# A retention kernel whose state product runs in 64x64 quarters of the array, with the state evicted by one instruction

## The chip, the cores and the metric

The kernel runs on one core of one Trainium2 chip. The metric is device time in microseconds (us); three runs of the kernel before gave 316.77, 317.41 and 318.12, so the median is 317.41 us. One further execution was profiled. All single durations below come from that execution.

## The reference

For 8 batches (B) and 8 heads (H), with 576 positions (S) and a head size of 64 (D), the reference computes decayed attention without a softmax and then an MLP with a cosine gate:

```python
scores = q @ k.T / sqrt(D)
Dmat   = where(i >= j, gamma[h] ** (i - j), 0)     # gamma[h] = 1 - 2**(-5-h)
ret    = (scores * Dmat) @ v                        # (B, H, S, D)
x      = ret.transpose(0, 2, 1, 3).reshape(4608, 512)
h      = x @ w_in                                   # 512 -> 2048
out    = (h * cos(h)) @ w_out                       # 2048 -> 512
```

Inputs and output are float32; the kernel multiplies in bfloat16 and accumulates in float32.

## The kernel before, in words

**Retention in chunks.** The decay factor of a pair (i, j) splits into a factor of i times a factor of j. The factor of j is multiplied into v when v is cast (tile VB, line 308), the factor of i into the result when it leaves PSUM (tile UP, line 476). Between the two the work is plain linear attention in chunks of 128 positions: r = 0 to 3 with 128 positions and r = 4 with 64. For each batch b and chunk r:

- `scores(b, r)`, line 405: 8 matmuls, one for each head, k against q with a contraction of 64. The two heads of a pair stand on partitions 0 to 63 and 64 to 127 (hp = 0 and 1), so their matmuls use the two row halves of the array (form 64\*128; for r = 4 it is 64\*64). They write two PSUM banks SC. VectorE then multiplies by the causal mask into RT (`mask`, line 426, instruction at line 428).
- `rest(b, r)`, line 433: for r > 0 first the product of the state S (the sum of k^T v over the earlier chunks of the batch) with q, then the 8 matmuls of RT with VB, both into bank PO; for r < 4 then 8 matmuls that add this chunk's k^T v to bank ST (lines 459 to 468), and ScalarE's eviction of ST into the bfloat16 tile SB (lines 469 to 474), which the next chunk's `rest` reads. VectorE moves PO, times UP, into XT (line 476), the transposed input of the MLP.

**The state in SB before.** SB is 128 partitions by 4 pairs of 128 columns. A pair's 128x128 block is block diagonal: head 0's 64x64 state top left, head 1's bottom right, and zeros elsewhere, set once at the start by two memsets (line 236). One matmul with contraction 128 and 128 output partitions (form 128\*128) so serves both heads of a pair: 4 matmuls for each `rest` with r > 0. There are 32 of those: 24 with 128 columns of q (r = 1 to 3) and 8 with 64 (r = 4). The eviction takes two ScalarE instructions of 64 partitions by 256 elements, one for each diagonal.

**The MLP.** Tokens go in 9 blocks j of 512. `mlp1(j, dt)` (line 489) makes one of 16 tiles of h with 4 matmuls of 512 columns; ScalarE takes the cosine into CB (line 504) and VectorE the product into GT (line 507). `mlp2(j, st, part)` (line 514) is one quarter of an output tile, again 4 matmuls of 512 columns; ScalarE evicts the finished tile (line 538) and issues its store. `mlp1` and `mlp2` take turns in four PSUM banks MM.

**The order.** It is written out by hand in `emit` (line 550), and each engine runs its instructions in that order. The helper classes add a semaphore wait where one engine reads what another wrote. PE's instructions are issued by `group` (line 396), so all matmuls have the lines 401 and 403 (the last one of a group, which raises the semaphore) and are told apart by their tiles: `po<-kqt,sb` is the state product, `po<-rt,vb` the product with RT, `st<-vb,kqb` the state's update, `sc<-kqt` the scores, `mm<-xt,win` mlp1, `mm<-wout,gt` mlp2. Waits of a group stand before its first matmul.

- Batch 0 runs at the start, while weights still arrive: `scores` and `rest` for r = 0 to 3 at lines 592 to 609, with `spin` matmuls (of the identity, result unused) between them, r = 4 inside `mlp1(0)` (lines 612 to 619). The pieces of w_in come by POOL's DMA queue; `mlp1(0)` waits for the piece that it reads (dt 0, 2, 4, 8, 12).
- Batch 1 runs inside `mlp2(0)` and `mlp1(1)` (lines 626 to 653). There the `mlp1` tiles have 320 columns at first and 192 after that.
- From j = 1 on (line 654), with b = j + 1: ahead of `mlp2(j)` stands `rest(b-1, 4)`, then `scores(b, 0)`; ahead of its quarters n = 3, 6, 9 and 12 stands `stage(b, r)`, which is `rest(b, r)` and `scores(b, r+1)` for r = 0 to 3. `mlp1(j)` for j > 1 has no retention work of PE. For j = 7, `rest(7, 4)` is the last retention work, with no scores after it; j = 8 has none.

Of the kernel before, what the change touches and what calls it, by code (L numbers as in the profile page):

```python
# [9 lines left out]
BF16 = mybir.dt.bfloat16  # L10
# [113 lines left out]
class _Kernel:  # L124
    def __init__(self, nc, es, q, k, v, w_in, w_out, out):
        self.nc, self.es = nc, es
        self.src = {"q": q.tensor, "k": k.tensor, "v": v.tensor}
        self.w_in, self.w_out, self.out = w_in.tensor, w_out.tensor, out.tensor
        gam = [1.0 - 2.0 ** (-5.0 - h) for h in range(H_)]
        self.lng = [math.log(g) for g in gam]  # L130
        self.s = Sched(nc, es)

        def sb(name, shape, dt):
            return nc.alloc_sbuf_tensor(name, shape, dt)


        self.KQT = [sb(f"kqt{i}", [128, TP], BF16) for i in range(2)]
        self.bQT = [[Buf() for _ in range(NCH)] for _ in range(2)]
        self.bKT = [[Buf() for _ in range(NCH)] for _ in range(2)]
        self.XT = sb("xt", [128, NP * XR], BF16)  # L140
        self.bXT = [Buf() for _ in range(XR // GR)]
        self.WIN = sb("win", [128, 4 * DFF], BF16)
        self.bWIN = [Buf() for _ in range(len(WI) - 1)]
        self.WOUT = sb("wout", [128, 16 * DM], BF16)
        self.bWOUT = [Buf() for _ in range(NWO)]
        self.ST32 = {x: [sb(f"{x}n{r}", [128, DM], F32) for r in range(NCH)] for x in "kv"}
        self.QN = sb("qn", [128, NCH * DM], F32)
        self.bQN = [Buf() for _ in range(NP)]
        self.bST32 = {x: [Buf() for _ in range(NCH)] for x in "kvq"}
        self.bQB = [[Buf() for _ in range(NCH)] for _ in range(2)]  # L150

        self.QX = [sb(f"qx{i}", [128, NP * S_], BF16) for i in range(2)]
        self.bQX = [Buf(), Buf()]
        self.bQ0 = [Buf() for _ in range(NP)]

        self.KQB = [[sb(f"kqb{i}_{r}", [128, 2 * DM], BF16) for r in range(NCH)] for i in range(2)]
        self.bKB = [[Buf() for _ in range(NCH)] for _ in range(2)]
        self.VB = [[sb(f"vb{i}_{r}", [128, DM], BF16) for r in range(NCH)] for i in range(2)]
        self.bVB = [[Buf() for _ in range(NCH)] for _ in range(2)]
        self.RT = [[sb(f"rt{i}_{hp}", [128, 512], BF16) for hp in range(2)] for i in range(2)]  # L160
        self.bRT = [[Buf() for _ in range(2)] for _ in range(2)]
        self.SB = [sb(f"sb{i}", [128, NP * 128], BF16) for i in range(2)]
        self.bSB = [Buf() for _ in range(2)]
        self.GT = [sb(f"gt{i}", [128, 16 * TB], BF16) for i in range(2)]
        self.bGT = [[Buf() for _ in range(16)] for _ in range(2)]
        self.CB = [sb(f"cb{i}", [128, TB], BF16) for i in range(3)]
        self.bCB = [Buf() for _ in range(3)]
        self.n_cb = 0
        self.NOSB = 4
        self.OSB = [sb(f"osb{i}", [128, DM], F32) for i in range(self.NOSB)]  # L170
        self.bOSB = [Buf() for _ in range(self.NOSB)]
        self.n_osb = 0
        self.IG = sb("ig", [128, S_], F32)
        self.IP = sb("ip", [128, NCH], F32)
        self.UP = sb("up", [128, NP * S_], F32)
        self.WV = sb("wv", [128, NCH * H_], F32)
        self.MK = sb("mk", [128, CH], BF16)
        self.ID = sb("ident", [128, 128], BF16)
        self.LNG = sb("lng", [128, NP], F32)
        self.JUNK = sb("junk", [128, 1], F32)  # L180
        self.C_LN8 = sb("c_ln8", [128, 1], F32)
        self.C_PIH = sb("c_pih", [128, 1], F32)
        self.bIG, self.bIP, self.bUP, self.bWV, self.bMK, self.bC, self.bID = (Buf() for _ in range(7))

        def ps(name):
            return nc.alloc_psum_tensor(name, [128, 512], F32)

        self.SC = [ps("sc0"), ps("sc1")]
        self.bSC = [Buf(), Buf()]
        self.PO, self.bPO = ps("po"), Buf()  # L190
        self.ST, self.bST = ps("st"), Buf()
        self.MM = [ps(f"mm{i}") for i in range(4)]
        self.bMM = [Buf() for _ in range(4)]
        self.n_mm = 0
        self.later = None
        self.stores = []
        self.fetched = 2 * NCH
        self.rt = {}
        self.open = {}
# [18 lines left out]
    def consts_a(self):  # L218

        s = self.s  # L220
        s.op("pool", lambda e: e.iota(self.IP.ap(), [[CH, NCH]], base=0, channel_multiplier=1,
                                      allow_small_or_imprecise_dtypes=True), writes=[self.bIP])
        for t, b, fill, first, cmp in ((self.ID, self.bID, 1.0, 0.0, ALU.not_equal),
                                       (self.MK, self.bMK, 0.0, 1.0, ALU.is_ge)):
            s.op("dve", lambda e: e.memset(t.ap(), first), writes=[b])
            s.op("pool", lambda e: e.affine_select(t.ap(), t.ap(), pattern=[[1, CH]],
                                                   compare_op=cmp, fill=fill, base=0,
                                                   channel_multiplier=-1), reads=[b], writes=[b])
        for h in range(H_):
            p0 = 64 * (h % 2)  # L230
            s.op("dve", lambda e: e.memset(bass.AP(self.LNG, p0 * NP + h // 2, [[NP, 64], [1, 1]]),
                                           self.lng[h]), writes=[Buf()])
        s.op("dve", lambda e: e.memset(self.C_LN8.ap(), float(math.log(1.0 / 8.0))), writes=[Buf()])
        s.op("dve", lambda e: e.memset(self.C_PIH.ap(), float(math.pi / 2.0)), writes=[self.bC])
        for i in range(2):
            s.op("dve", lambda e: e.memset(self.SB[i].ap(), 0.0), writes=[self.bSB[i]])
        for h in range(H_):
            s.op("act", lambda e: e.activation(
                bass.AP(self.WV, h, [[NCH * H_, 128], [H_, NCH]]), self.IP.ap(), AF.Exp,
                scale=-self.lng[h]), reads=[self.bIP], writes=[Buf()])  # L240
        self.bWV.w = [Tok("act", "act", s.count["act"], {})]
# [188 lines left out]
            bass.AP(self.MK, 0, [[CH, ck], [0, NP], [1, ck]]), ALU.mult),  # L430
            reads=[sc[1], self.bMK], writes=[self.bRT[k][hp]])

    def rest(self, b, r, po=None):

        s, ck, i, q0 = self.s, ck_of(r), b % 2, CH * r
        k = self.rt[b, r]
# [1 line left out]
        mms = []  # L438
        if r:
            sb = self.SB[(r - 1) % 2]  # L440
            mms += [(bass.AP(po, c * CH, [[512, 128], [1, ck]]),
                     bass.AP(sb, c * 128, [[512, 128], [1, 128]]),
                     bass.AP(self.KQT[i], TQ + c * S_ + q0, [[TP, 128], [1, ck]]),
                     dict(start=c == 0, stop=False, skip_group_check=True)) for c in range(NP)]
        for c in range(NP):
            for hp in range(2):
                h = 2 * c + hp
# [9 lines left out]
        if r < NCH - 1:  # L457
            mms = []
            for c in range(NP):
                for hp in range(2):  # L460
                    h = 2 * c + hp
                    mms.append((
                        bass.AP(self.ST, 64 * hp * 512 + c * D_, [[512, 64], [1, D_]]),
                        bass.AP(self.KQB[i][r], h * D_, [[2 * DM, ck], [1, D_]]),
                        bass.AP(self.VB[i][r], h * D_, [[DM, ck], [1, D_]]),
                        dict(start=r == 0 and c == 0, stop=r == NCH - 2 and c == NP - 1,
                             skip_group_check=True)))
            self.group(mms, [self.bKB[i][r], self.bVB[i][r]], [self.bST])
            for hp in range(2):

                s.op("act", lambda e: e.activation(  # L471
                    bass.AP(self.SB[r % 2], 64 * hp * 512 + 64 * hp, [[512, 64], [128, NP], [1, D_]]),
                    bass.AP(self.ST, 64 * hp * 512, [[512, 64], [D_, NP], [1, D_]]), AF.Copy),
                    reads=[self.bST], writes=[self.bSB[r % 2]] if hp else [Buf()])
        t0 = (b * S_ + q0) % XR
        s.op("dve", lambda e: e.tensor_tensor(  # L476
            bass.AP(self.XT, t0, [[NP * XR, 128], [XR, NP], [1, ck]]),
# [72 lines left out]
    def emit(self):  # L550
# [61 lines left out]
        for dt in range(16):  # L612
# [3 lines left out]
            if dt == 4:  # L616
                self.scores(0, 4)
            if dt == 6:
                self.rest(0, 4)

        self.fetch(2)
        for r in range(NCH):
# [31 lines left out]
        for j in range(1, NTB):  # L654
# [5 lines left out]
            for n in range(16):  # L660

                if n == 0 and b <= B_:
                    self.rest(b - 1, NCH - 1)
                if b < B_:
                    if n == 0:
                        self.scores(b, 0)
                    elif n % 3 == 0 and n < 15:
                        self.stage(b, n // 3 - 1)
                self.mlp2(j, n // 4, n % 4)
        self.flush()  # L670
# [31 lines left out]
```

## Time and profile before

| what | value |
|---|---|
| median of three runs | 317.41 us (316.77 to 318.12) |
| the profiled execution: its own time | 316.4 us |
| span of its trace | 314.7 us |
| granted clock of TensorE | 1.0 over the whole span |
| busy: PE, DVE, ACT, POOL | 303.5, 174.1, 162.3, 93.1 us |
| the eviction into SB (line 471) | 64 instructions, 378 ns each |
| state product, 128 columns of q | 92 records, 219 ns each |
| state product, 64 columns of q | 32 records, 193 ns each |

A span on PE is modelled: a matmul's recorded length covers its way through the array, and the next one starts long before it ends. What PE pays for a matmul is therefore read from the distance between starts: 216 ns from one 512-column matmul to the next, 56 ns for 128 columns. In the text, "gap" is such a distance. (Four more state products of 128 columns stand in the trace under the tile `mm`.) Single matmul records are missing from the trace, and such a place shows a gap that is one matmul too long.

### The profile page before, as it was taken

What the parts mean: (1) busy time and instruction counts of PE and PEld (TensorE: products, weight loads), DVE (VectorE), ACT (ScalarE), POOL (GpSimd) and SP (SyncE); (2) the same over time, 40 slices, a digit from 0 to 9 for tenths busy, and PEclk for the clock granted to TensorE, in tenths of its full rate; (3) what the DMA queues carried; (4) which work ended last, traced back from release to release, by engine and by line L of the source; (5) the groups of instructions that cost most, each with busy time, mean ns of one, the idle gap of its engine ahead of it and who ended that gap; (6) DMA issues with size and microseconds to landing.
All of it is one profiled execution on the core that took longest, in us unless ns stands there. A gap on an engine that the chain in (4) does not pass through costs nothing.

```text
span 314.7 us, 6424 instructions
## 1 busy us (share of the span) xinstructions
PE 303.5 (96%) x2516; PEld 159.6 (51%) x2552; DVE 174.1 (55%) x301; ACT 162.3 (52%) x290; POOL 93.1 (30%) x128
## 2 busy tenths in 40 slices
PE   6989999999999999999999999999999999999996
PEld 5754455666544455445544554455444544444442
DVE  3567624787527743685458644765387438405700
ACT  7566525785337533763277236723473257316711
POOL 2692027535454434453445424210000000000000
PEclk9999999999999999999999999999999999999999
DMA  7999999999999999999999999940001100120021
GB/s 218 213 168 204 203 220 247 264 192 209 212 256 183 217 210 247 217 224 217 259 208 202 225 204 221 172 85 35 33 0 38 66 33 0 42 94 1 12 83 74
DMA packets 142814, 48.85 MB, mean 155 GB/s; under 512 B 132544, under 2 KB 137664, under 8 KB 142784
## 3 DMA queue, kind: packets, MB, share of 16 engines
q1 hardware_dynamic: 132320, 34.22, 59.7%
q0 software_dynamic: 5280, 4.78, 9.5%
q10 hardware_dynamic: 5184, 9.44, 8.9%
q8 instruction: 20, 0.33, 0.4%
q14 instruction: 10, 0.08, 0.1%
HBM read 36.70 MB, written 9.44 MB: 147 GB/s over the span
## 4 chain that ended last, share of the span: by engine, by line
PE 90%; DMA 2%; DVE 2%; ACT 2%; issue 2%; SPq 1%; POOL 0%; DVEq 0%
PE mm L401 59%; PE mm L403 20%; PE po L401 6%; PE sc L401 4%; DMA kn<-in_k_dram 2%; PE st L401 1%; DVE gt L507 1%; DVE rt L428 1%; SPq L276 1%; ACT sb L471 0%; DVE xt L476 0%; ACT L604 0%; ACT osb L538 0%; ACT kqt L365 0%; SPq L267 0%
## 5 line engine op out<-in xcount | busy, mean ns | idle before, releaser
L507 DVE TENSOR_TENSOR gt<-mm,cb 128x512 bf16<-128x512 f32 (+2 forms) x160 | 101.1, 637 | 66.2 <-ACT cb L504 63.6
L401 PE MATMUL mm<-xt,win 128*128 128x512 bf16 (+2 forms) x468 | 116.0, 358 | 1.0 <-DVE xt L476 0.3
L504 ACT ACTIVATE cb<-mm,c_pih 128x512 bf16<-128x512 f32 (+2 forms) x160 | 101.9, 645 | 27.8 <-PE mm L403 27.0
L401 PE MATMUL mm<-wout,gt 128*128 128x512 bf16 x408 | 111.8, 380 | 2.3 <-issue 1.7
L401 PEld LDWEIGHTS mm<-xt,win 128*128 128x128 bf16 x480 | 44.6, 98 | 48.8 <-DVE gt L507 2.3
L401 PEld LDWEIGHTS mm<-wout,gt 128*128 128x128 bf16 x432 | 39.3, 98 | 45.1
L403 PE MATMUL mm<-xt,win 128*128 128x512 bf16 (+2 forms) x160 | 57.2, 358 | 0.3
L538 ACT ACTIVATE osb<-mm 128x512 f32<-128x512 f32 x36 | 21.5, 597 | 68.0 <-PE mm L403 68.0
L403 PE MATMUL mm<-wout,gt 128*128 128x512 bf16 x144 | 54.6, 379 | 0.5
L308 POOL TENSOR_TENSOR vb<-vn,wv 128x512 bf16<-128x512 f32 (+1 forms) x40 | 41.7, 1043 | 29.2 <-DMA vn<-in_v_dram 24.7
L428 DVE TENSOR_TENSOR rt<-sc,mk 128x512 bf16<-128x512 f32 (+1 forms) x78 | 45.8, 625 | 4.8 <-PE sc L403 4.8
L476 DVE TENSOR_TENSOR xt<-po,up 128x512 bf16<-128x512 f32 (+1 forms) x39 | 24.7, 634 | 41.9 <-PE po L403 41.8
L471 ACT ACTIVATE sb<-st 64x256 bf16<-64x256 f32 x64 | 24.2, 378 | 40.1 <-PE st L403 38.7
L318 POOL CAST kqb<-kn 128x512 bf16<-128x512 f32 (+1 forms) x40 | 24.4, 611 | 65.2 <-DMA kn<-in_k_dram 56.2
L318 POOL CAST kqb<-qn 128x512 bf16<-128x512 f32 (+1 forms) x30 | 18.5, 615 | 17.7 <-DMA qn<-in_q_dram 17.5
L403 PEld LDWEIGHTS mm<-xt,win 128*128 128x128 bf16 x160 | 15.7, 98 | 15.7
L403 PEld LDWEIGHTS mm<-wout,gt 128*128 128x128 bf16 x144 | 14.1, 98 | 17.0
L401 PE MATMUL po<-rt,vb 128*64 128x128 bf16 (+1 forms) x273 | 15.2, 220 | 0.0
L401 PE MATMUL sc<-kqt 64*128 64x128 bf16 (+1 forms) x273 | 14.7, 215 | 0.0
L401 PEld LDWEIGHTS po<-kqt,sb 128*128 128x128 bf16 x124 | 8.6, 98 | 7.8 <-DVE rt L428 1.6
L401 PEld LDWEIGHTS po<-rt,vb 128*64 128x64 bf16 (+1 forms) x273 | 9.3, 108 | 5.9 <-DVE rt L428 2.1
L401 PE MATMUL po<-kqt,sb 128*128 128x128 bf16 (+1 forms) x124 | 11.2, 213 | 0.4 <-DVE rt L428 0.2
(88 smaller groups left out, 133.2 us busy)
## 6 DMA issues: line engine op xcount, KB each, us to landing
out_dram<-osb ACTq DMA_DIRECT2D x36, 256.0 KB, 3.3
kn<-in_k_dram SPq DMA_DIRECT2D x32, 256.0 KB, 4.7
vn<-in_v_dram SPq DMA_DIRECT2D x32, 256.0 KB, 5.3
qn<-in_q_dram SPq DMA_DIRECT2D x24, 256.0 KB, 4.8
wout<-in_moe_w_out_dram POOLq DMA_DIRECT2D x4, 512.0 KB, 14.5
win<-in_moe_w_in_dram POOLq DMA_DIRECT2D x3, 512.0 KB, 8.2
qn<-in_q_dram SPq DMA_DIRECT2D x4, 288.0 KB, 4.7
kn<-in_k_dram SPq DMA_DIRECT2D x8, 128.0 KB, 3.5
```

Source lines behind the costliest of these rows:

```text
L276: s.dma("sp", f"q0_{c}", lambda e: e.dma_start(dst, src), writes=[self.bQN[c]])
L308: self.s.op(eng, lambda e: e.tensor_tensor(bass.AP(self.VB[i][r], 0, v3), self.staged("v", r, v3[1:]), bass.AP(self.WV, r * H_, [[NCH * H_ ...
L318: self.s.op(eng, lambda e: e.tensor_copy(o, f), reads=[self.bST32[x][r]], writes=[bt[i][r]])
L401: self.nc.tensor.matmul(o, a, b, **kw)
L403: return s.done("pe", self.nc.tensor.matmul(o, a, b, **kw), reads, writes)
L428: self.s.op("dve", lambda e: e.tensor_tensor(bass.AP(self.RT[k][hp], 0, p3), bass.AP(sc[0], 0, p3), bass.AP(self.MK, 0, [[CH, ck], [0, NP] ...
L471: s.op("act", lambda e: e.activation(bass.AP(self.SB[r % 2], 64 * hp * 512 + 64 * hp, [[512, 64], [128, NP], [1, D_]]), bass.AP(self.ST, 6 ...
L476: s.op("dve", lambda e: e.tensor_tensor(bass.AP(self.XT, t0, [[NP * XR, 128], [XR, NP], [1, ck]]), bass.AP(po, 0, [[512, 128], [CH, NP], [ ...
L504: s.op("act", lambda e: e.activation(co, mo, AF.Sin, bias=self.C_PIH.ap(), scale=1.0), reads=[bm, self.bC], writes=[bcb])
L507: s.op("dve", lambda e: e.tensor_tensor(bass.AP(g, dt * TB + o, [[16 * TB, 128], [1, n]]), mo, co, ALU.mult), reads=[bm, bcb], writes=[bg])
L538: s.op("act", lambda e: e.activation(o.ap(), m.ap(), AF.Copy), reads=[bm], writes=[bo])
```

## The change

SB shrinks to 4 pairs of 64 columns: partitions 0 to 63 hold the states of the heads hp = 0, partitions 64 to 127 those of hp = 1, packed side by side, exactly as they lie in ST. So one ScalarE instruction of 128 partitions by 256 elements evicts both, and the two memsets go. The state product becomes 8 matmuls for each `rest` with r > 0, one for each head: contraction 64, 64 output partitions, with hp = 0 in the quarter of rows 0 to 63 and columns 0 to 63 and hp = 1 in the opposite quarter (form 64\*64).

For r = 4, whose RT product uses the rows 0 to 63 with both column halves (64\*64), `rest` gets an argument `mid`: the state product is issued as a group of its own, then `mid()` issues other PE work, then PE waits for its own semaphore until the state product is complete, then the RT product follows. For batches 1 to 6 `mid` is `scores(b, 0)`, which stood after `rest` before; for batches 0 and 7 it is one spin matmul, which is new and takes an MM bank. The group of the state product for r = 4 thus waits only for SB, q and PO; the wait for RT and VB moves behind `mid`. On VectorE, the two masks of `scores(b, 0)` come ahead of the XT instruction of `rest(b-1, 4)` instead of after it.

```diff
-        self.SB = [sb(f"sb{i}", [128, NP * 128], BF16) for i in range(2)]
+        self.SB = [sb(f"sb{i}", [128, NP * D_], BF16) for i in range(2)]
...
-        for i in range(2):
-            s.op("dve", lambda e: e.memset(self.SB[i].ap(), 0.0), writes=[self.bSB[i]])
...
-    def rest(self, b, r, po=None):
+    def rest(self, b, r, po=None, mid=None):
...
-            mms += [(bass.AP(po, c * CH, [[512, 128], [1, ck]]),
-                     bass.AP(sb, c * 128, [[512, 128], [1, 128]]),
-                     bass.AP(self.KQT[i], TQ + c * S_ + q0, [[TP, 128], [1, ck]]),
-                     dict(start=c == 0, stop=False, skip_group_check=True)) for c in range(NP)]
+            mms += [(bass.AP(po, 64 * hp * 512 + c * CH, [[512, 64], [1, ck]]),
+                     bass.AP(sb, 64 * hp * NP * D_ + c * D_, [[NP * D_, 64], [1, D_]]),
+                     bass.AP(self.KQT[i], 64 * hp * TP + TQ + c * S_ + q0, [[TP, 64], [1, ck]]),
+                     dict(start=c == 0, stop=False, skip_group_check=True))
+                    for c in range(NP) for hp in range(2)]
+        if mid:
+            done = self.group(mms, [self.bSB[(r - 1) % 2], self.bQT[i][r]], [bpo])
+            mid()
+            s.eng["pe"].wait_ge(s.sem["pe"], done.val)
+            mms = []
...
-            for hp in range(2):
-                s.op("act", lambda e: e.activation(
-                    bass.AP(self.SB[r % 2], 64 * hp * 512 + 64 * hp, [[512, 64], [128, NP], [1, D_]]),
-                    bass.AP(self.ST, 64 * hp * 512, [[512, 64], [D_, NP], [1, D_]]), AF.Copy),
-                    reads=[self.bST], writes=[self.bSB[r % 2]] if hp else [Buf()])
+            s.op("act", lambda e: e.activation(
+                self.SB[r % 2].ap(), self.ST[:, 0:NP * D_], AF.Copy),
+                reads=[self.bST], writes=[self.bSB[r % 2]])
...
-                self.rest(0, 4)
+                self.rest(0, 4, mid=lambda: self.spin(1))
...
-                    self.rest(b - 1, NCH - 1)
+                    self.rest(b - 1, NCH - 1, mid=(lambda: self.scores(b, 0)) if b < B_
+                              else (lambda: self.spin(1)))
                 if b < B_:
-                    if n == 0:
-                        self.scores(b, 0)
-                    elif n % 3 == 0 and n < 15:
+                    if n % 3 == 0 and 0 < n < 15:
                         self.stage(b, n // 3 - 1)
```

## The prediction

> **What bounds the kernel now.** I read the page first, busy times and chain:
>
> ```profile
> PE 303.5 (96%) x2516; PEld 159.6 (51%) x2552; DVE 174.1 (55%) x301; ACT 162.3 (52%) x290; POOL 93.1 (30%) x128
> PE 90%; DMA 2%; DVE 2%; ACT 2%; issue 2%; SPq 1%; POOL 0%; DVEq 0%
> PE mm L401 59%; PE mm L403 20%; PE po L401 6%; PE sc L401 4%; DMA kn<-in_k_dram 2%; PE st L401 1%; DVE gt L507 1%; DVE rt L428 1%; SPq L276 1%; ACT sb L471 0%; DVE xt L476 0%; ACT L604 0%; ACT osb L538 0%; ACT kqt L365 0%; SPq L267 0%
> ```
>
> PE is busy 96% of the span and 90% of the chain; ScalarE's eviction of the state (ACT sb L471) rounds to 0% of it. What ScalarE saves is then worth something only where PE waits for it; what PE has to do more is paid in full wherever PE runs without a gap. So the next view is PE's timeline of one steady stage, batch 3, r = 2:
>
> ```profile
> 116.87 0.38 PE L403 MATMUL mm<-wout,gt 128*128 128x512 bf16 x1
> 117.09 0.39 PE L401 MATMUL po<-kqt,sb 128*128 128x128 bf16 x4
> 117.41 0.41 PE L401 MATMUL po<-rt,vb 128*64 128x128 bf16 x7
> 117.60 0.22 PE L403 MATMUL po<-rt,vb 128*64 128x128 bf16 x1
> 117.65 0.29 PE L401 MATMUL st<-vb,kqb 128*64 128x64 bf16 x7
> 117.75 0.20 PE L403 MATMUL st<-vb,kqb 128*64 128x64 bf16 x1
> 117.88 0.39 PE L401 MATMUL sc<-kqt 64*128 64x128 bf16 x7
> 118.06 0.22 PE L403 MATMUL sc<-kqt 64*128 64x128 bf16 x1
> 118.21 0.61 PE L401 MATMUL mm<-wout,gt 128*128 128x512 bf16 x2
> ```
>
> The starts of the single records (ns) give gaps. mm to state product 216, the normal 512-column distance: PE waits for nothing, and both have form 128\*128. Inside the state product 56, 55, 56. Then 149 to the first RT product, whose form is 128\*64: 93 more than 56. Inside that, two heads start 3 to 4 apart and pairs follow at 56 (the second pair at 80), 195 from first to last start. st follows at 53 (same form); sc, form 64\*128, at 128 where 28 would follow; mm at 148. So **every change of form costs about 93 to 100 ns**: the next form starts only once the last one is through. The change needs two more rows: form 64\*64 after 128\*128, and form 64\*64 in opposite quarters. The turning of q in batch 1 has both:
>
> ```profile
> 42.85 0.38 PE L403 MATMUL mm<-wout,gt 128*128 128x512 bf16 x1
> 43.16 0.47 PE L401 MATMUL po<-ident,qx 64*64 64x64 bf16 x17
> ```
>
> Gap 309 (216 + 93); inside, the two quarters of a pair start 3 ns apart, the second pair 52 after the first, the others at 32, a 64-column stream's price.
>
> **The change part by part.**
>
> *State product, r = 1 to 3.* Before, from the last mm start to the first RT product: 216 + 167 + 149 = 532. After: mm to 64\*64 309; four pairs at the RT product's own pattern (same columns, also pairs on disjoint column halves) 195; to form 128\*64 149, since that again differs: 653. **+120 ns.** Eight matmuls in pairs take four slots, as four full ones did: the zeros that go were never paid for, and one change of form is added. Batches 2 to 7, 18 times: **+2.16 us**. In batch 1, r = 1 waits 469 for ScalarE's turned k (end 53.65) in bank PO, which hides the change of form: +0.02; r = 2 and 3 wait for their second mask (gap 180, where 136 would be normal) and start at 136 + 93 = 229: +0.07 each. Together **+0.15**.
>
> *r = 4, batches 1 to 6.* Before: 216 + 87 (state) + 123 + 119 (RT) + 125 + 181 (scores) + 148 to the first mm = 999. After: 309 + 119 (state, the 64-column pattern of form 64\*64) + 125 + 181 (scores) + 148 + 119 (RT) + 125 = 1126. +0.127, six times: **+0.76**. That takes the wait for PE's own semaphore as hidden. Behind it on PE stand the RT product and all of mlp2. The state product's end is 193 after its last start; consumers start 58 to 99 after the end they wait for (the state product at 14.517 after the mask's end at 14.459; the one at 19.114 after ScalarE's end at 19.015). So release is at 251 to 292, while scores hold the array until 125 + 181 + 148 = 454: 160 to spare. If PE released only once the scores were through as well, it would be 216 + 58 instead of 148: +0.13 each, +0.76 in all, the upper bound; below nothing it cannot go.
>
> *r = 4, batch 7,* has one spin as cover. Before 216 + 86 + 124 + 119 + 125 = 670; after 309 + 119 + X + 119 + 125 with X between 125 + 149 = 274 (two changes of form) and 292 (the release): **+0.28**. *Batch 0, r = 4* waits today for its second mask (start 27.91, mask's end 27.85). Its state product, freed of that wait, goes ahead at 27.69, the spin at 27.93, RT at about 28.08 against 28.13: 0. The spin's MM bank has been emptied by then (gt of dt = 3 ends at 26.1), and the next tiles find theirs empty too.
>
> *The eviction.* Which form will it cost like? The groups kept apart by form say:
>
> ```profile
> L471 ACT ACTIVATE sb<-st 64x256 bf16<-64x256 f32 x64 | 24.2, 378 | 40.1 <-PE st L403 38.7
> L365 ACT ACTIVATE kqt<-mm 128x256 bf16<-128x256 f32 x2 | 0.8, 376 | 0.0
> ```
>
> Same elements in a partition, twice the partitions, same time: 32 instructions of 0.38 us go, 12 us of ScalarE. In the steady stages SB is ready at about 118.8 for a reader at 120.8: worth 0. It stands on the chain once, at the start (chain in order of time):
>
> ```profile
> 18.34 0.27 ACT sb L471
> 18.61 0.03 issue
> 18.64 0.39 ACT sb L471
> 19.02 0.09 issue
> 19.11 0.72 PE mm L401 x11
> ```
>
> There `rest(0, 3)` would start some 0.37 earlier (from 18.64 the masks, ready at 18.61, are next to be waited for). But what is late next is a DMA: the first piece of w_in lands at 20.41, just ahead of mlp1(0) at 20.64, so at most 0.13 is left there, and the third piece lands at 24.52; PE's wait for it ends, and dt = 4 starts at 24.66:
>
> ```profile
> 24.63 0.34 PEld L401 LDWEIGHTS mm<-xt,win 128*128 128x128 bf16 x3 [0.54 <-DVE gt L507]
> ```
>
> The gt named as releaser can only be the one that ended at 24.05 (the next ends at 24.92), in time for an unhindered start at 24.42; the weights were what came last. POOL issues that piece, and nothing of POOL changes. So the gain ends here: **0**, and the changes of form in batch 0 end here too, with 0.24 to spare. Without this cover it would be -0.37.
>
> *The rest.* The two memsets (272 ns each, until 2.65) precede a VectorE wait for q until 4.78: 0. On VectorE, XT of `rest(b-1, 4)` falls behind two masks and ends at about 109.7 in batch 3's stage, as the second mask does now; the reader of both starts at 109.97, after the change 0.13 later: covered by 0.2. Queues of SP and POOL do not change.
>
> **Sum:** 2.16 + 0.15 + 0.76 + 0.28 = **+3.35 us**. The profiled execution took 316.4 with a span of 314.7; it would be 319.75 and 318.0. That execution lies 1.0 under the median 317.41, to which I add the same: **320.8**.
>
> A page speaks against the pairs: the Trainium skill, "TensorEngine Tiling (Array Packing)", Gotcha 1, says that different row tiles cannot write one PSUM bank at the same time. Both quarters of a pair are different row tiles and write PO. The turning of q also writes one bank from both row halves, in opposite column halves, 3 ns apart, so I go by the row; by the page the time would be the second rival's.
>
> **The rivals.**
>
> 1. *Not slower:* the change of form from 64\*64 to 128\*64 costs nothing. Its place is between state and RT product for r = 1 to 3; both forms share the column halves, and this direction is nowhere in the trace. It would give 56 instead of 149, -93 ns 21 times, -1.95: +1.40, **318.8**, within 0.5%. It decides from a gap of about 65 on. Against it: the opposite direction (st 128\*64 to sc 64\*64, 126 where 28 would follow) pays in full, as does each other pair of forms.
> 2. *Pairs in series.* Eight slots instead of four: about +0.22 for 128 columns, 21 times, +0.10 for 64, 7 times: +5.3 more, **326.1**. Against it the 3 ns above.
> 3. *The own wait exposed:* +0.76, **321.5**. For it: no such wait is in the trace. Against it: 160 ns of cover.
> 4. *The eviction does what it says in time:* the start keeps its 0.37 because w_in lands sooner, **320.4**; or, the change not doing what it says, one eviction costs as much as two: ScalarE keeps its time, and the forecast stays, since nothing rests on it.
>
> **How the numbers follow.** Forecast with rival 4: 0.80; rival 1: 0.08; rivals 2 and 3: 0.05 each; 0.02 is left for what no row shows. The range leaves out rival 2 and takes in 1 and 3 with the spread of the runs shown (0.7 each side of the median): 318.7 to 322.0. 0.5% is 1.6 us, about what a measurement of this kernel can tell from no change. Slower by over that: the forecast and rivals 2 and 3, 0.90. Within: rival 1, 0.08. Faster: those 0.02.
>
> **What would show it.** Right: gap 309 ahead of `po<-kqt,sb` of form 64\*64, 195 inside it, 149 after it; mlp2(1) about 0.3 later than now; the following distance between mlp1 stages 0.49 longer (3 x 120 + 127); `sb<-st` 32 times at 378. Wrong: a gap of 56 after it (1), starts 56 apart singly (2), RT of r = 4 more than 150 after the scores (3), the 24.66 start moved forward (4).

## The result, and the profile after

The changed kernel takes 320.19 us (median of 6 runs, 320.06 to 320.65); the kernel before, run beside it, 316.99 (6 runs, 316.43 to 318.12). The ratio is 1.010 with a 95% interval of 1.0081 to 1.0119: slower by 2.6 to 3.8 us, 3.20 by the medians, where +3.35 was forecast. (The 320.8 of the forecast starts from 317.41, the median of the three runs known then, 0.42 above the 316.99 here.) Page of the profiled execution after (its own time 320.2, span 318.4), busy times and chain:

```profile
PE 307.7 (97%) x2643; PEld 159.2 (50%) x2682; DVE 173.7 (55%) x299; ACT 150.7 (47%) x258; POOL 92.9 (29%) x128
PE 89%; DMA 5%; issue 1%; DVE 1%; SPq 1%; ACT 1%; POOL 0%; DVEq 0%
```

Against the page before, ScalarE lost 11.6 us of busy time and PE gained 4.2. The time followed PE. The same steady stage as before, batch 3, r = 2, on PE's timeline (line numbers have moved by a few; L399 and L401 are the two lines of `group`):

```profile
118.20 0.38 PE L401 MATMUL mm<-wout,gt 128*128 128x512 bf16 x1
118.50 0.41 PE L399 MATMUL po<-kqt,sb 64*64 64x128 bf16 x8
118.85 0.41 PE L399 MATMUL po<-rt,vb 128*64 128x128 bf16 x7
...
119.65 0.39 PE L399 MATMUL mm<-wout,gt 128*128 128x512 bf16 x1
```

In the single records the state product starts 309 ns after the last mm (216 before), its eight starts span 195 (167 before), its two quarters start 3 to 4 ns apart, and RT follows at 146 (149 before). From the last mm to RT that is 650 instead of 532: +118 ns, forecast 120. Ahead of mlp2(2), r = 4 of batch 2 in its new order:

```profile
107.36 0.38 PE L401 MATMUL mm<-xt,win 128*128 128x512 bf16 x1
107.67 0.31 PE L399 MATMUL po<-kqt,sb 64*64 64x64 bf16 x7
...
107.91 0.39 PE L399 MATMUL sc<-kqt 64*128 64x128 bf16 x7
...
108.24 0.31 PE L399 MATMUL po<-rt,vb 64*64 64x64 bf16 x7
...
108.48 0.39 PE L399 MATMUL mm<-wout,gt 128*128 128x512 bf16 x1
```

The gaps are 309, 119 inside, 125 to the scores, 182 inside, 146 to RT, 119 inside, 125 to mm: 1125 instead of 999. RT starts 146 ns after the last score, as RT does behind the state product above, where PE waits for no semaphore of its own: in r = 4 that wait is not seen.

The evictions, groups kept apart by form:

```profile
L475 ACT ACTIVATE sb<-st 128x256 bf16<-128x256 f32 x32 | 12.3, 384 | 42.7 <-PE st L401 42.7
```

32 at 384 ns replace 64 at 378.

### The profile page after: what moved, and what is told of

It is laid out like the page before. It is cut to its first block, busy times and chain, and to the rows that moved or that the text cites. A ratio compares the mean times of both kernels' runs of the same rounds, so it can differ in the third digit from the quotient of the medians.

```text
span 318.4 us, 6639 instructions
## 1 busy us (share of the span) xinstructions
PE 307.7 (97%) x2643; PEld 159.2 (50%) x2682; DVE 173.7 (55%) x299; ACT 150.7 (47%) x258; POOL 92.9 (29%) x128
## 4 chain that ended last, share of the span: by engine, by line
PE 89%; DMA 5%; issue 1%; DVE 1%; SPq 1%; ACT 1%; POOL 0%; DVEq 0%
PE mm L399 58%; PE mm L401 20%; PE po L399 7%; PE sc L399 3%; DMA vn<-in_v_dram 2%; DMA win<-in_moe_w_in_dram 2%; DVE gt L510 1%; PE st L399 1%; SPq L274 1%; SPq L265 0%; ACT osb L541 0%; POOL vb L306 0%; ACT cb L507 0%; ACT kqt L363 0%; POOL kqb L316 0%
## 5 line engine op out<-in xcount | busy, mean ns | idle before, releaser
L399 PE MATMUL mm<-xt,win 128*128 128x512 bf16 (+2 forms) x471 | 116.8, 358 | 1.5 <-DMA win<-in_moe_w_in_dram 1.0
L399 PE MATMUL mm<-wout,gt 128*128 128x512 bf16 x404 | 111.1, 380 | 2.1 <-issue 1.3
L399 PEld LDWEIGHTS mm<-xt,win 128*128 128x128 bf16 x480 | 44.6, 98 | 49.4 <-DVE gt L510 1.9
L399 PEld LDWEIGHTS mm<-wout,gt 128*128 128x128 bf16 x432 | 39.3, 98 | 44.7
L401 PE MATMUL mm<-xt,win 128*128 128x512 bf16 (+2 forms) x159 | 56.9, 358 | 0.3
L401 PE MATMUL mm<-wout,gt 128*128 128x512 bf16 x143 | 54.2, 379 | 0.4
L475 ACT ACTIVATE sb<-st 128x256 bf16<-128x256 f32 x32 | 12.3, 384 | 42.7 <-PE st L401 42.7
L401 PEld LDWEIGHTS mm<-xt,win 128*128 128x128 bf16 x160 | 15.7, 98 | 15.7
L401 PEld LDWEIGHTS mm<-wout,gt 128*128 128x128 bf16 x144 | 14.1, 98 | 17.0
L399 PE MATMUL po<-rt,vb 128*64 128x128 bf16 (+1 forms) x273 | 15.2, 220 | 0.0
L399 PE MATMUL sc<-kqt 64*128 64x128 bf16 (+1 forms) x273 | 14.7, 215 | 0.0
L399 PEld LDWEIGHTS po<-kqt,sb 64*64 64x64 bf16 x240 | 7.3, 106 | 12.5 <-issue 10.8
L399 PE MATMUL po<-kqt,sb 64*64 64x128 bf16 (+1 forms) x240 | 11.9, 217 | 0.4 <-DVE rt L426 0.2
L399 PEld LDWEIGHTS po<-rt,vb 128*64 128x64 bf16 (+1 forms) x273 | 9.3, 108 | 6.0 <-DVE xt L479 2.1
```

The source lines that it names most:

```text
L399: self.nc.tensor.matmul(o, a, b, **kw)
L401: return s.done("pe", self.nc.tensor.matmul(o, a, b, **kw), reads, writes)
L475: s.op("act", lambda e: e.activation(self.SB[r % 2].ap(), self.ST[:, 0:NP * D_], AF.Copy), reads=[self.bST], writes=[self.bSB[r % 2]])
```

## The experiments

All times stand against the kernel before, run on the same chip: median 316.78 (29 runs) for the first four, 316.39 (14 runs) for the last two. Theory F says that what is paid is changes of form on PE. The rivals, each with a letter, are named in the expectations. "The trace" of an experiment is one profiled execution.

**1. Eight matmuls without the new form.** On the kernel before, for r = 1 to 3:

```diff
-            mms += [(bass.AP(po, c * CH, [[512, 128], [1, ck]]),
-                     bass.AP(sb, c * 128, [[512, 128], [1, 128]]),
...
+            else:
+                mms += [(bass.AP(po, 64 * hp * 512 + c * CH, [[512, 64], [1, ck]]),
+                         bass.AP(sb, c * 128 + 64 * hp, [[512, 128], [1, 64]]),
...
+                        for c in range(NP) for hp in range(2)]
```

> The kernel before with one edit: for r = 1 to 3 the state product is 8 matmuls of form 128*64 (contraction 128, the block-diagonal state cut into its two column halves), the form of the RT product behind it; r = 4, the evictions and the order stay. Theory F (each change of form on PE costs about 95 ns, the number of matmuls nothing as long as they run in pairs): the change of form only moves from behind the state product to ahead of it: gap 309, 195 inside, 53 after it, +25 ns a chunk, so +0.3 us against before (batch 1 gains 0.1). Rival M (eight small matmuls cost more than four full ones in themselves, whatever their form): like the changed kernel, +2.3 us.

Measured: 316.71 (12 runs), ratio 0.9991 (0.9969 to 1.0012). Eight matmuls instead of four cost nothing here, so rival M, which asked for +2.3 us, is out. PE's timeline of this kernel, batch 3, r = 2:

```profile
116.96 0.38 PE L403 MATMUL mm<-wout,gt 128*128 128x512 bf16 x1
117.27 0.41 PE L401 MATMUL po<-kqt,sb 128*64 128x128 bf16 x8
117.52 0.39 PE L401 MATMUL po<-rt,vb 128*64 128x128 bf16 x7
```

The gaps are 309 ns ahead of the state product, 195 inside, and 52 to RT, which has the same form and runs on: the change of form has moved, and RT's own starts now span 171 instead of 195. The expected +25 ns a chunk was wrong by that: the late second pair (24 ns) belongs to the first group of a form, so it is paid once. The sum from the last mm to the last RT start is 727 ns in both kernels.

**2. The eviction in two again.** On the changed kernel:

```diff
-            s.op("act", lambda e: e.activation(
-                self.SB[r % 2].ap(), self.ST[:, 0:NP * D_], AF.Copy),
-                reads=[self.bST], writes=[self.bSB[r % 2]])
+            for hp in range(2):
+                s.op("act", lambda e: e.activation(
+                    self.SB[r % 2][64 * hp:64 * hp + 64, :],
+                    self.ST[64 * hp:64 * hp + 64, 0:NP * D_], AF.Copy),
+                    reads=[self.bST], writes=[self.bSB[r % 2]] if hp else [Buf()])
```

> The changed kernel with the eviction taken apart again: two ScalarE instructions of 64 partitions by 256 elements, one for each half of the compact state. Theory F (the eviction is nowhere last to arrive): the steady stages stay as in the changed kernel to the nanosecond, so +3.2 us against before, with what the arrival of the first weights varies (0.5 us). Rival E (the single eviction gives something back that hides a larger cost of the quarters): later than the changed kernel by 0.38 us wherever PE waits for it, over +5 us against before if it is each steady chunk.

Measured: 320.12 (6 runs), ratio 1.0093 (1.0066 to 1.0119), where the changed kernel, beside its own runs of the kernel before, has 1.0100 (1.0081 to 1.0119). In the steady stages nothing changes (table below), so rival E, with its +5 us, is out. In batch 1 this execution has 0.48 us more than the changed kernel's: from the first mm of mlp1(1) to that of mlp2(1) it loses 0.70 against before, the changed kernel 0.22. There the view of what PE's weight loads wait for (time, times, longest), of this kernel and then of the changed one, reads:

```profile
PEld mm L399 <- ACT cb L509: 2.1, 7, 0.4
```

```profile
PEld mm L399 <- DVE gt L510: 1.8, 7, 0.4
```

In that stretch PE waits for banks, and the last to come is ScalarE's cosine instead of VectorE's product. ScalarE's timeline at the state of chunk 2, of this kernel and then of the changed one, shows part of the reason:

```profile
60.98 0.78 ACT L476 ACTIVATE sb<-st 64x256 bf16<-64x256 f32 x2 [0.29 <-PE st L401]
61.78 0.94 ACT L509 ACTIVATE cb<-mm,c_pih 128x320 bf16<-128x320 f32 x2
```

```profile
60.78 0.38 ACT L475 ACTIVATE sb<-st 128x256 bf16<-128x256 f32 x1 [0.28 <-PE st L401]
61.42 1.07 ACT L507 ACTIVATE cb<-mm,c_pih 128x320 bf16<-128x320 f32 x2 [0.26 <-PE mm L401]
```

With two evictions the cosine starts right behind the second (also in the kernel before); with one it waits 0.26 for PE instead. Counted from the start of mlp1(1), at the first tile of 192 columns this kernel is 0.18 behind the changed one; the other 0.30 come up in the sixteen tiles of 192 columns, where no eviction stands, and why is not settled by any run. The medians show no such loss, but their intervals are too wide to rule out 0.48.

**3. The new order alone.** On the kernel before, r = 4 keeps its full-size product, but takes `mid`, the scores or spin in it, and the wait:

```diff
+        if mid:
+            done = self.group(mms, [self.bSB[(r - 1) % 2], self.bQT[i][r]], [bpo])
+            mid()
+            s.eng["pe"].wait_ge(s.sem["pe"], done.val)
+            mms = []
```

> The kernel before with the new order of r = 4 alone: the full-size state product (128*128, block diagonal) as a group of its own, then scores or a spin, then PE's wait for its own semaphore, then RT. Theory F: batches 1 to 6 have the same three changes of form as before (128*128 to 64*128, to 64*64, to 128*128) and the wait is hidden: 216 + 87 + 125 + 181 + 148 + 119 + 125 = 1001 ns against 999, 0; batch 7 waits for its own semaphore, +0.15. In all +0.15 us against before. Rival W (the own wait and the new order cost): +0.13 to +0.25 us in each of the six, +0.8 to +1.5 us.

Measured: 316.58 (12 runs), ratio 0.9996 (0.9972 to 1.0021). In the trace the r = 4 of the batches with scores lie within 2 ns of before, that of batch 7 costs +128 ns (expected 150). Rival W is out. PE's timeline of this kernel at r = 4 of batch 2:

```profile
106.90 0.39 PE L401 MATMUL sc<-kqt 64*128 64x128 bf16 x7
107.08 0.22 PE L403 MATMUL sc<-kqt 64*128 64x128 bf16 x1
107.23 0.31 PE L401 MATMUL po<-rt,vb 64*64 64x64 bf16 x7
```

RT follows the last score at 146 here too. The wait shows only in batch 7, where a single spin of the state product's own form is all the cover:

```profile
269.88 0.19 PE L403 MATMUL po<-kqt,sb 128*128 128x64 bf16 x1
269.90 0.22 PE L403 MATMUL mm<-ident 128*128 128x128 bf16 x1
270.13 0.31 PE L401 MATMUL po<-rt,vb 64*64 64x64 bf16 x7
```

RT starts 223 ns after the spin and 252 after the last start of the state product. In the changed kernel's batch 7 the spin has another form than both its neighbours, and RT starts 160 after it.

**4. The quarters for r = 1 to 3 alone.** On the kernel before, with one eviction into a compact SB after r = 0 to 2, and a block-diagonal tile SD of its own for r = 4:

```diff
+            if r == NCH - 1:
+                mms += [(bass.AP(po, c * CH, [[512, 128], [1, ck]]),
+                         bass.AP(self.SD, c * 128, [[512, 128], [1, 128]]),
...
+            else:
+                mms += [(bass.AP(po, 64 * hp * 512 + c * CH, [[512, 64], [1, ck]]),
+                         bass.AP(sb, 64 * hp * NP * D_ + c * D_, [[NP * D_, 64], [1, D_]]),
...
```

> The quarters for r = 1 to 3 alone, with the single eviction for r = 0 to 2; r = 4 as before, with a block-diagonal state of its own that is evicted by two instructions after r = 3, and the old order. Theory F: the 18 steady chunks at +0.12 us and 0.15 in batch 1, +2.3 us against before, so 0.9 to 1.0 below the changed kernel, since r = 4 (six at 0.126 and one at 0.287 in the changed kernel's trace) goes back to before. Rival W (most of the loss stands in r = 4 with its wait): under +1 us.

Measured: 319.23 (12 runs), ratio 1.0069 (1.0049 to 1.0088), so +1.5 to +2.8. Rival W, which asked for under +1 us, is out here too. In the trace each steady batch loses 353 ns, 3 x 118, and r = 4 loses nothing. Batch 3, r = 2, on PE's timeline, with the gaps of the changed kernel:

```profile
117.40 0.38 PE L404 MATMUL mm<-wout,gt 128*128 128x512 bf16 x1
117.71 0.41 PE L402 MATMUL po<-kqt,sb 64*64 64x128 bf16 x8
118.05 0.41 PE L402 MATMUL po<-rt,vb 128*64 128x128 bf16 x7
```

With experiment 3 this gives the parts of the +2.69 in the table below: 1.77 for the quarters of r = 1 to 3, 0.13 for the order (measured with the full-size product), and by difference 0.79 for the quarters' form in r = 4.

**5. Fewer changes of form than before.** On the kernel before:

```diff
-        if r + 1 < NCH:
-            self.scores(b, r + 1)
+        if r == 1:
+            self.scores(b, 2)
+            self.scores(b, 3, sc=[self.bank(), self.bank()])
+        if r == 3:
+            self.scores(b, 4)
...
                         self.scores(b, 0)
+                        self.scores(b, 1, sc=[self.bank(), self.bank()])
```

> The kernel before (full-size state product) with fewer changes of form: for batches 2 to 7 the scores of chunks 0 and 1 stand together ahead of mlp2, those of 2 and 3 together behind chunk 1 (the second of each two in two MM banks), those of 4 behind chunk 3 as before; three RT buffers instead of two. Theory F: two changes of form a batch go (scores to mm after chunk 0 and after chunk 2), 98 ns each, 12 in all: -1.2 us against before, 315.6 where before has 316.8, a ratio near 0.9963. Rival B (banks or VectorE): the masks come in fours and the mlp2 tiles wait for banks, so the time stays or grows, 0 to +1 us.

Measured: 315.21 (9 runs), ratio 0.9956 (0.9940 to 0.9971), -1.2 us by the medians: faster than both kernels. Rival B is out. PE's timeline of this kernel ahead of mlp2(2), the second scores (into MM banks) right behind the first:

```profile
107.26 0.39 PE L401 MATMUL sc<-kqt 64*128 64x128 bf16 x7
107.44 0.22 PE L403 MATMUL sc<-kqt 64*128 64x128 bf16 x1
107.50 0.38 PE L401 MATMUL mm<-kqt 64*128 64x128 bf16 x7
```

53 ns from the last score of one chunk to the first of the next, where a change costs 128 and 148. A batch gains 213 ns.

**6. The quarters beside a neighbour of their form.** On the changed kernel, for r = 3 the state product goes behind the state's update, ahead of the scores of chunk 4, which are 64\*64 too:

```diff
+        if r == NCH - 2 and b > 1:
+            last, mms = [(*m[:3], dict(start=False, stop=m is mms[-1], skip_group_check=True)) for m in mms], []
...
             self.group(mms, [self.bKB[i][r], self.bVB[i][r]], [self.bST])
+            if last:
+                self.group(last, reads[3:], [bpo])
```

> The changed kernel, where for r = 3 of batches 2 to 7 the state product of form 64*64 comes last in rest, right ahead of the scores of chunk 4, which are 64*64 as well; RT's product opens the bank instead. Theory F: one change of form less in each (from the last mm to the first score 1025 ns instead of 1118, and the scores' second pair no longer starts late, another 24): -0.117 us six times, -0.7 us against the changed kernel, so +2.6 to +2.7 against before. Rival M (quarters cost in themselves, wherever they stand): as the changed kernel, +3.3 to +3.4.

Measured: 319.09 (6 runs), ratio 1.0074 (1.0050 to 1.0098), 2.7 us over before by the medians and 120 ns a batch under the changed kernel in the trace. The same quarters cost less once they share a form with what follows, so rival M is out again, by the trace: the medians alone, with 0.5 us of change, would not decide it. PE's timeline of this kernel, batch 3, r = 3:

```profile
123.29 0.30 PE L399 MATMUL po<-kqt,sb 64*64 64x128 bf16 x4
123.37 0.21 PE L399 MATMUL sc<-kqt 64*64 64x64 bf16 x1
123.42 0.22 PE L399 MATMUL po<-kqt,sb 64*64 64x128 bf16 x2
```

The first score starts before the last state products, though it stands behind them in program order. By the kernel's addresses the scores of the heads hp = 1 use rows 64 to 127 with columns 0 to 63, a quarter that the state product leaves free.

**The steady stretch in one table.** From the first recorded mm of mlp1(2) to that of mlp2(8), which holds five batches of the new order and no arrival of weights. "Expected" counts changes of form from the gaps of the trace before.

| kernel | us | against before | expected |
|---|---|---|---|
| before | 205.00 | | |
| changed | 207.69 | +2.69 | 15 x 0.120 + 5 x 0.127 + 0.28 = +2.72 |
| 1, full column halves | 205.00 | 0.00 | 15 x 0.025 = +0.38 |
| 2, two evictions | 207.69 | +2.68 | +2.69, as changed |
| 3, order only | 205.13 | +0.13 | +0.15 |
| 4, quarters r = 1 to 3 | 206.77 | +1.77 | 15 x 0.120 = +1.80 |
| 5, scores in pairs | 203.94 | -1.07 | -5 x 0.196 = -0.98 |
| 6, state beside scores | 207.09 | +2.09 | 2.69 - 5 x 0.117 = +2.11 |

## Why the prediction was right, step by step

- **State product, r = 1 to 3.** Forecast +120 ns, measured +118. The direction that no row showed, 64\*64 to 128\*64, pays in full (146), so rival 1 is out. Experiment 1 shows the cause: eight matmuls in the form of RT are free.
- **Pairs.** They start 3 to 4 ns apart in one bank, as the turning of q had it; rival 2 is out. What the prediction cites from the Trainium skill, "TensorEngine Tiling (Array Packing)", Gotcha 1, that different row tiles cannot write one PSUM bank at the same time, does not hold here: two row halves whose column halves differ start into bank PO 3 to 4 ns apart, with the next pair 56 to 80 behind, and rival 2's +5.3 us did not come.
- **r = 4.** Forecast +127, measured +126; the own wait is hidden, as 160 ns of cover said, and rival 3 is out. Batch 7: forecast 0.28, measured 0.287.
- **Batch 1.** Forecast 0.15 and 0.127 for its r = 4, measured 0.01 up to the start of mlp1(1) and 0.22 from there to mlp2(1), 0.04 less in all. The prediction did not look for the eviction here. Experiment 2 shows that here the second eviction does hold up a cosine; what one eviction is worth in this stretch, between nothing and some tenths of a us, is open.
- **The eviction.** Worth nothing in the steady stages, as forecast: experiment 2 undoes it and the stretch stays. At the start the step was wrong in its middle: the masks were said to be next to be waited for, at 18.61. Next is POOL's vb of chunk 3, which ends at 18.97 before and at 18.92 after. Groups by form, of the changed kernel:

```profile
L399 PE MATMUL mm<-kqt,sb 64*64 64x128 bf16 x8 | 0.4, 218 | 0.6 <-POOL vb L306 0.6
```

So `rest(0, 3)` starts at 19.07 instead of 19.11: 0.05 of the 0.37 were there to be had, not all of it. In the five executions with two evictions the second ends at most 0.18 after that vb (experiment 5), so rival 4's 0.37 was not there in any of them. The sum wasn't touched: it had 0 here.
- **The start.** In the profiled execution after, mlp2(0) starts 0.49 later than in the one before. Its chain in order of time:

```profile
13.82 7.37 DMA win<-in_moe_w_in_dram
21.19 0.35 issue
```

The first piece of w_in landed at 21.19 instead of 20.41, though POOL issued it at nearly the same time (13.82 against 13.86). It is not that landing alone: in experiment 2 the piece lands at 20.26, ahead of before, and mlp2(0) still starts 0.55 later, behind a piece of v that took 8.61 us to land. Against the execution before, mlp2(0) starts at -0.11, +0.31 and +0.53 in the experiments that keep the block-diagonal state there (3, 1, 5) and at -0.13, +0.55 and +1.09 in the quartered ones (4, 2, 6). So it varies about as much from execution to execution as between the kernels, and the 0.49 isn't put down to the change; whether a few tenths are, these eight traces cannot tell. Between the two profiled executions the rest, 3.77 - 0.49 = 3.28, stands against the forecast of 3.35. So mlp2(1), for which the prediction named about 0.3, starts 0.73 later, 0.49 of it from here. The distance between the mlp1 stages that follow grows by 0.48, where it named 0.49.

Not tried: r = 4 with RT right behind the quarters and no wait between. Both are 64\*64, but the two row halves would then write the same column half of PO with nothing to order them.

## What to carry to other kernels

Before a product is cut into smaller pieces, count the changes of form around it on PE's timeline: here the zeros in a full-size product cost nothing (four matmuls 56 ns apart, or four pairs 56 ns apart after a first step of 80), while each change of form cost 93 to 100 ns. Group work of one form instead (experiment 5: two changes a batch less, 1.2 us). And time saved on an engine that is not the last to arrive stays on that engine: of the 11.6 us of ScalarE the steady stages got nothing and the start at most 0.05; only in batch 1 is its worth open.

## What was not expected of the hardware

- The 24 ns by which the second pair comes late after a change of form belong to the first group in that form only (RT's starts span 195 ns behind another form, 171 behind its own).
- In one form, matmuls of two groups in different quarters overlap out of their groups' order (experiment 6). The chunk was 3 ns cheaper than the count said (120 instead of 117).
- The first piece of w_in lands 5.6 to 7.7 us after its issue in these eight traces, with nothing changed in the loads, and mlp2(0) starts over a spread of 1.2 us. The steady stretch, by contrast, is 207.69 in the changed kernel and in experiment 2, 7 ns apart.
